# Sparse attention and a gated feed-forward layer: how the fourth tile's attention output is transposed, and the order of the work around it

## The chip, the cores and the metric

The kernel runs on one core of one Trainium2 chip. The metric is the device time of one execution in microseconds (us), lower is better. A core has a matrix engine (TensorE, PE in the profile; its weight loads are listed as PEld), two elementwise engines (VectorE, DVE; ScalarE, ACT), GpSimd (POOL), which here adds rows and issues the loads, and SyncE (SP), which issues DMA transfers. Each engine takes its instructions strictly in order; semaphores tie the engines together. Matrix products land in PSUM, everything else lies in SBUF.

## The reference

Attention over 4 batches, 8 heads, 768 positions of width 64, followed by a feed-forward layer on 3072 rows of width 512 (hidden width 2048):

```python
k_sum = k.reshape(B, H, nb, block, D).max(axis=3)      # blocks of 32 keys
v_sum = v.reshape(B, H, nb, block, D).mean(axis=3)
scores_l = scale * q @ k^T, kept only where |i - j| < 16
scores_s = scale * q @ k_sum^T + log(32)
a = softmax(concat(scores_l, scores_s))
attn = a @ concat(v, v_sum)
x = attn, heads side by side, as [3072, 512]
h = x @ w_in
out = (h * clip(h + 3, 0, 6) / 6) @ w_out
```

Inputs and output are float32; the kernel works in bfloat16 with float32 accumulation.

## The kernel before, in words

**Tiles.** The 3072 rows are eight tiles of 384 (s = 0 to 7: batch s // 2, half s % 2); "the fourth tile" is s = 3. For a tile the attention gives x, kept transposed in SBUF (`x`, 128 x 4 x 384: the width on the partitions), because the first product (`f1`, L703) needs it so. That product has 16 groups `F{s}x{ft}`: four matmuls into one of three PSUM accumulators `h`, then on ScalarE the clamp from below (L707), then on VectorE the upper clamp and the product with h, which writes `g` (L708) and frees the accumulator. The second product (`f2`, L720) takes `g` to the output: per 128 rows four parts `G{s}{ts}x0.0` to `.3` of four matmuls each into the one accumulator `o`, a copy to SBUF (`.4`) and a store by SyncE (`.5`).

**Attention of a batch.** Loads by GpSimd (`K`, `Q`, `V`, `H` and `B` entries); block transposes of keys and queries on VectorE (`turn`, L461 and L465), the block maxima (L473) and their spreading; value sums (`vsum`, `u` entries: for the later batches additions on GpSimd, L567, then spreads over the windows by ScalarE or VectorE); scores of half a batch for four heads at a time (`scores4`, L518: 48 small matmuls), the exponential on ScalarE (L526) and the mask on VectorE (L527).

**Value products and the transpose of x.** `values` (L646, entries `v{b}{half}{g}`, batches counted from 0: the fourth tile's are v110 and v111) makes for half a tile's width g the value products (`.0`, L660: 24 matmuls), the reciprocal of the sums (`.1`, L635) and the scaled rows `xn` (`.2`, L642). Then there are two ways to turn `xn` into x:

- tiles s < LATE: six identity matmuls on TensorE (`.3`, L673) into PSUM and one copy from there to x (`.4`, L247, by ScalarE or VectorE);
- tiles s >= LATE: VectorE transposes blocks of 32 x 32 in place of the whole (`.3`, L679) into `y`, and SyncE moves the blocks to their partitions: after both halves, four entries `.4` to `.7` of the second half g = 1, four transfers each (L685), sixteen for a tile. The tile's first products wait for all sixteen.

**What sets the order.** A list of 1000 entries written out by hand, ORDER, is walked from front to back; each entry emits one operation on its engine, and a letter behind a colon (A, D) picks ScalarE or VectorE where either could do it. Each engine so gets its own order, and buffers are given to whoever comes first in the list. [...]

Of the kernel before, what the change touches and what calls it, by code (L numbers as in the profile page):

```python
# [15 lines left out]
D = 64  # L16
# [27 lines left out]
F1x12.0 F1x12.1 F1x12.2 O0.0 G02x0.0 F1x10.0 F1x10.1 Q1w5.0 F1x10.2 Q1w3.0 O1.0 q4.0 q5.0 G02x0.1 F1x3.0 F1x6.0 q5.1:A q4.1:A  # L44
s100.0 F1x3.1 w13.0 F1x6.1 w12.0 F1x11.0 O2.0 s100.1 O3.0 F1x3.2 w12.2 F1x6.2 s100.3 w13.2 w12.3:D G02x0.2 s101.0 G02x0.3
s101.1 F1x13.0 G02x0.4:A V10.0 s100.2 s101.3 w13.3:A F1x0.0 G00x0.0 w12.1:D G00x0.1 V12.0 K20.0 w13.1:A h110.0:A s110.0 F1x0.1
Q22.0 s110.3 K22.0 s110.1 K21.0 s100.4 G00x0.2 K23.0 G00x0.3 s101.2 u4.0 G00x0.4:A h130.0:D Z.0 h100.0:D F1x0.2 s110.4 G01x0.0
G01x0.1 G01x0.2 B2.2 G01x0.3 s110.2 H2.0 Q20.0 u4.1:A Q23.0 u4.2:D u4.5:A u4.3:D F1x13.1 u4.4:D F1x11.1 F1x11.2 F1x13.2 v100.0
h120.0:A v101.0 v100.1 v100.2 G01x0.4:A v101.1 h131.0:A G12x0.0 v101.2 G12x0.1 G12x0.2 h121.0:A v100.3 w21.0 v101.3 v101.4:D
v100.4:A G12x0.3 h111.0:A s111.0 G12x0.4:A s111.1 w20.0 F2x1.0 F2x1.1 V22.0 h101.0:A B2.3 F2x3.0 F2x2.0 w21.3 B2.0 F2x3.1  # L50
G10x0.0 w23.0 F2x2.1 F2x1.2 w23.3 Q21.0 G10x0.1 s111.3 G00x0.5 F2x3.2 B2.1 w20.2:A F2x2.2 F2x14.0 w22.0 w21.4:A F2x5.0 G10x0.2
F2x14.1 F2x15.0 w23.4:A K30.0 V20.0 F2x5.1 F2x14.2 s111.2 F2x11.0 F2x15.1 F2x5.2 G10x0.3 F2x13.0 F2x11.1 s111.4 w23.2:A F2x15.2
F2x10.0 w22.2:A s101.4 u5.0 F2x11.2 F2x4.0 F2x13.1 K32.0 G10x0.4:A w20.3 v111.0 F2x13.2 v110.0 F2x4.1 w21.1 F2x4.2 v110.1
v111.1 F2x12.0 v110.2 v111.2 G11x0.0 G11x0.1 F2x0.0 F2x12.1 w22.1 K33.0 w20.1 w21.2:A F2x10.1 v111.3 F2x0.1 v111.4:A F2x0.2
u5.1 w21.5:A v110.3 u5.2 w20.5:A F2x12.2 v110.4:A u5.3 H2.1:A G12x0.5 G11x0.2 F2x10.2 G11x0.3 F2x8.0 u5.4 w20.4:A G11x0.4:A
G10x0.5 F2x6.0 F3x5.0 F2x6.1 Q30.0 u5.5 w23.1 F2x8.1 w22.3 F3x5.1 F2x6.2 s200.0 G22x0.0 u5.6 F2x8.2 F3x5.2 u5.7 s200.1 Q33.0
F2x7.0 u5.8 s200.3 F2x9.0 w22.4:D u5.9:D F2x7.1 F2x7.2 F2x9.1 u5.11:D s210.0 F2x9.2 F3x9.0 F3x14.0 G22x0.1 u5.12:D F3x13.0
s210.3 s200.2 s210.4 s210.1 F3x14.1 F3x9.1 G11x0.5 u5.10:A F3x14.2 F3x9.2 F3x13.1 G22x0.2 s200.4 Q31.0 s210.2 F3x13.2 F3x4.0
v201.0 v200.0 v201.1 F3x8.0 G22x0.3 F3x4.1 v201.2 G22x0.4:A F3x4.2 K31.0 Q32.0 v200.1 F3x7.0 v200.2 F3x12.0 F3x7.1 v201.3
G20x0.0 v200.3 s201.0 w23.5:A G20x0.1 F3x8.1 G20x0.2 F3x8.2 G20x0.3 F3x12.1 s201.1 w22.5:A s201.3 G20x0.4:A F3x12.2 F3x7.2  # L60
w30.0 B3.3 w31.0 F3x0.0 F3x2.0 F3x0.1 w30.3 G22x0.5 s211.0 F3x0.2 F3x3.0 B3.1 F3x2.1 G21x0.0 s201.2 w31.2:A v201.5 w33.0 F3x1.0
s211.1 F3x3.1 F3x1.1 F3x3.2 s211.3 G21x0.1 s201.4 F3x2.2 G21x0.2 F3x1.2 s211.4 F3x6.0 w31.3 F3x6.1 w30.2:A v201.6 G21x0.3
s211.2 w31.1 F3x10.0 F3x6.2 w33.3 H3.0 v201.4 F3x10.1 w31.4:A w30.4:A B3.0 B3.2 v211.0 v201.7 v210.0 G20x0.5 F3x11.0 V30.0
V32.0 G21x0.4:A u6.0 G21x0.5 F3x10.2 F3x15.0 F3x11.1 F3x15.1 F3x11.2 v211.1 F3x15.2 w30.1 G32x0.0 w30.5:D v211.2 G32x0.1 v210.1
u6.1 G32x0.2 w31.5:A H3.1:A F4x15.0 v210.2 F4x15.1 F4x7.0 G32x0.3 F4x4.0 F4x15.2 u6.2 F4x2.0 G01x0.5 F4x7.1 w33.4:D G32x0.4:A
F4x7.2 F4x2.1 F4x4.1 v210.3 F4x8.0 F4x8.1 v211.3 u6.3 F4x4.2 G30x0.0 G30x0.1 F4x2.2 F4x8.2 F4x6.0 s300.0 v211.6 w32.1 F4x6.1
v211.5 F4x14.0 u6.4 F4x14.1 F4x5.0 F4x5.1 u6.5 F4x6.2 w33.1 F4x13.0 F4x14.2 s300.1 G30x0.2 u6.6 w32.0 u6.7 F4x5.2 F4x3.0
F4x13.1 w33.2:A G30x0.3 F4x3.1 F4x12.0 u6.8 G30x0.4:A s300.3 F4x13.2 w32.2:D F4x3.2 w32.3 w32.4:D s300.2 F4x0.0 u6.11:D F4x0.1
F4x12.1 F4x11.0 F4x12.2 G31x0.0 u6.10:D w33.5:D G31x0.1 F4x11.1 s310.0 v211.7 u6.9:D F4x0.2 u6.12:D F4x1.0 F4x11.2 G31x0.2
F4x10.0 F4x9.0 s310.1 v211.4 w32.5:D F4x1.1 s300.4 s310.3 G31x0.3 s310.2 s310.4 F4x1.2 G02x0.5 F4x10.1 F4x9.1 v301.0 v300.0  # L70
F5x14.0 F4x10.2 F4x9.2 G31x0.4:A v301.1 F5x14.1 G30x0.5 v300.1 G42x0.0 v300.2 F5x5.0 F5x14.2 v301.2 v300.3 F5x2.0 F5x4.0 s301.0
F5x2.1 G42x0.1 F5x2.2 G42x0.2 v301.3 G31x0.5 F5x5.1 F5x9.0 s301.1 v301.7 F5x4.1 F5x5.2 F5x9.1 v301.6 s301.3 F5x0.0 F5x4.2
F5x9.2 F5x0.1 F5x6.0 s301.2 F5x0.2 G42x0.3 s311.0 F5x3.0 F5x6.1 F5x6.2 F5x1.0 s311.1 G42x0.4:D F5x3.1 G40x0.0 v301.4 F5x13.0
v301.5 F5x1.1 s311.2 F5x3.2 s311.3 F5x1.2 G40x0.1 s301.4 s311.4 F5x13.1 F5x10.0 v310.0 F5x13.2 v311.0 v310.1 v310.2 F5x7.0
F5x7.1 F5x7.2 v311.1 F5x8.0 F5x8.1 F5x8.2 F5x10.1 F5x10.2 G40x0.2 F5x12.0 G40x0.3 G40x0.4:A G42x0.5 F5x15.0 F5x11.0 v310.3
v311.2 v311.3 v311.7 F5x11.1 G32x0.5 G41x0.0 G41x0.1 G41x0.2 F5x11.2 F5x15.1 F5x15.2 F6x14.0 F5x12.1 F5x12.2 F6x14.1 F6x14.2
# [87 lines left out]
def kernel(  # L164
# [683 lines left out]
```

## Time and profile before

| what | value |
|---|---|
| time, median of 3 runs | 216.33 us (215.77 to 216.93) |
| the profiled execution's own time | 215.64 us |
| its span, first to last instruction | 213.9 us |
| PE busy | 207.7 us (97%) |
| DVE busy | 162.4 us (76%) |
| ACT busy | 131.2 us (61%) |
| POOL busy | 75.6 us (35%) |
| granted TensorE clock | 1.000 |

The profile is one execution. Busy time of an engine counts its instructions, not its waits on semaphores; matmuls overlap in the array, so from a timeline the price of a group of matmuls is read from the start of the group to the start of the next. The table by stretches gives each engine's busy time within a window. The chain of waits follows the work that ended last back to the front, and its pieces follow each other in time.

### The profile page before, as it was taken

Reading aid. Unit: us, or ns where it says so; the run is one execution under the profiler, and the core shown is the slowest. Engines: PE = TensorE matmul, PEld = TensorE weight load, DVE = VectorE, ACT = ScalarE, POOL = GpSimd, SP = SyncE. Lnnn points to the kernel's source line nnn. Section 1 sums busy time; section 2 is a strip of 40 time slices with the busy share of each in tenths; the row PEclk is TensorE's granted clock in tenths of the full one; section 3 lists DMA queues with packets and bytes.
Section 4 is the critical chain, followed back from the end, with each engine's and each line's share of the span. In section 5 each row is a group of like instructions: output and inputs, shape, how many; then the busy total and the mean of one; then the engine's idle time right before and its main releaser. Section 6 shows DMA issues by size and latency. Waiting matters only on the chain.

```text
span 213.9 us, 5917 instructions
## 1 busy us (share of the span) xinstructions
PE 207.7 (97%) x2444; PEld 118.4 (55%) x2444; DVE 162.4 (76%) x314; ACT 131.2 (61%) x266; POOL 75.6 (35%) x93
## 2 busy tenths in 40 slices
PE   7988999999999999999999999999999999999994
PEld 7556666655545555555555555555555555564443
DVE  6976999899199999999999999978865555650021
ACT  3869978888896867976664486375345355520110
POOL 7968358935743199980891000000000000000000
PEclk9999999999999999999999999999999999999999
DMA  5999999999999994899965033413314400113123
GB/s 76 157 155 187 204 187 171 190 204 163 183 196 182 193 164 43 115 178 167 171 57 161 9 39 44 134 16 39 72 21 78 78 0 11 41 49 123 52 82 139
DMA packets 92363, 24.23 MB, mean 113 GB/s; under 512 B 82480, under 2 KB 89008, under 8 KB 92336
## 3 DMA queue, kind: packets, MB, share of 16 engines
q0 software_dynamic: 62928, 15.99, 77.0%
q1 hardware_dynamic: 29264, 7.80, 16.2%
q8 instruction: 19, 0.31, 0.6%
q10 hardware_dynamic: 144, 0.07, 0.1%
q14 instruction: 8, 0.07, 0.1%
HBM read 31.97 MB, written 6.29 MB: 179 GB/s over the span
## 4 chain that ended last, share of the span: by engine, by line
PE 65%; DVE 24%; DMA 3%; ACT 2%; issue 2%; POOL 2%; DVEq 0%; POOLq 0%
PE h L703 29%; PE o L720 23%; DVE g L708 6%; PE h L720 5%; DVE at L527 4%; DMA first<-in_q_dram 3%; DVE kaug L461 3%; DVE xn L642 2%; DVE red L473 2%; DVE vaug L247 2%; DVE qT L465 2%; PE S L518 2%; PE S L660 1%; POOL first L311 1%; PE S L703 1%
## 5 line engine op out<-in xcount | busy, mean ns | idle before, releaser
L703 PE MATMUL h<-x,win 128*128 128x384 bf16 x500 | 92.2, 326 | 0.3
L707 ACT ACTIVATE r<-h 128x384 f32<-128x384 f32 x125 | 58.7, 491 | 42.1 <-PE h L703 40.0
L720 PE MATMUL o<-wout,g 128*128 128x512 bf16 x336 | 81.6, 379 | 0.0
L708 DVE SCALAR_TENSOR_TENSOR g<-r,h 128x384 bf16<-128x384 f32 x125 | 65.4, 544 | 18.2 <-ACT r L707 16.1
L703 PEld LDWEIGHTS <-win 128*128 128x128 bf16 x512 | 48.7, 98 | 36.6 <-issue 0.9
L720 PEld LDWEIGHTS <-g 128*128 128x128 bf16 x416 | 38.7, 98 | 37.5
L526 ACT ACTIVATE at<-S 120x768 bf16<-120x768 f32 x24 | 19.0, 810 | 4.2 <-PE S L518 4.2
L247 ACT COPY ot<-o 128x512 f32<-128x512 f32 x17 | 9.9, 585 | 16.5 <-PE o L720 16.3
L527 DVE TENSOR_TENSOR at<-at,mask 96x768 bf16<-96x768 bf16 x24 | 14.9, 645 | 0.5 <-ACT at L526 0.4
L642 DVE TENSOR_TENSOR xn<-S,rc 128x768 bf16<-128x768 f32 x14 | 13.2, 952 | 0.2
L247 DVE COPY ot<-h 128x512 f32<-128x512 f32 (+1 forms) x3 | 1.6, 554 | 14.3 <-PE h L720 14.3
L349 POOL DMA_DIRECT2D vaug<-in_v_dram x10 | 11.9, 1197 | 0.7 <-DMA qraw<-in_q_dram 0.4
L567 POOL TENSOR_TENSOR first<-first 128x512 f32<-128x512 f32 (+2 forms) x8 | 9.6, 1202 | 7.0 <-DMA first<-in_v_dram 6.4
L567 POOL TENSOR_TENSOR own<-own 128x512 f32<-128x512 f32 (+2 forms) x8 | 9.2, 1154 | 6.9 <-DMA own<-in_v_dram 6.5
L720 PE MATMUL h<-wout,g 128*128 128x128 bf16 (+2 forms) x80 | 11.4, 294 | 0.0
L473 DVE TENSOR_REDUCE red<-kaug 128x24 bf16<-128x768 bf16 x12 | 11.1, 928 | 0.0
L247 ACT COPY vaug<-vaug 32x640 bf16<-32x640 bf16 (+3 forms) x20 | 10.6, 579 | 0.8 <-ACT qT L247 0.7
L816 PE MATMUL o<-idle 128*128 128x64 bf16 (+2 forms) x71 | 7.4, 281 | 1.1 <-DVE idle L293 1.1
L461 DVE STREAM_TRANSPOSE kaug<-kraw 128x768 bf16<-128x768 bf16 x8 | 8.0, 1018 | 0.0
L660 PEld LDWEIGHTS <-at 120*64 120x64 bf16 x336 | 6.1, 111 | 3.1 <-issue 1.7
L518 PEld LDWEIGHTS <-kaug 32*128 32x128 bf16 x576 | 5.3, 92 | 4.4 <-issue 4.1
L679 DVE STREAM_TRANSPOSE y<-xn 128x768 bf16<-128x768 bf16 x8 | 7.5, 962 | 0.0
(117 smaller groups left out, 196.1 us busy)
## 6 DMA issues: line engine op xcount, KB each, us to landing
out_dram<-ot SPq DMA_DIRECT2D x19, 256.0 KB, 2.3
vaug<-in_v_dram POOLq DMA_DIRECT2D x6, 384.0 KB, 13.5
wout<-in_moe_w_out_dram POOLq DMA_DIRECT2D x4, 512.0 KB, 9.8
win<-in_moe_w_in_dram POOLq DMA_DIRECT2D x3, 512.0 KB, 9.9
kraw<-in_k_dram POOLq DMA_DIRECT2D x8, 192.0 KB, 11.0
x<-y SPq DMA_DIRECT2D x64, 24.0 KB, 2.1
first<-in_k_dram POOLq DMA_DIRECT2D x6, 192.0 KB, 13.5
first<-in_q_dram POOLq DMA_DIRECT2D x6, 192.0 KB, 10.6
```

The lines of the kernel that those rows point to most:

```text
L247: {"ACT": nc.scalar.copy, "DVE": nc.vector.tensor_copy, "POOL": nc.gpsimd.tensor_copy}[eng](o, i)
L349: op("POOL", "dma128", lambda: nc.gpsimd.dma_start(out=o[BLK:WIN, a:z, 0:D], in_=rows[:, a:z]), w=[("v", b % 2, c) for c in range(lo, hi)] ...
L461: op("DVE", "turn", lambda: nc.vector.transpose(out=w[:, :, BLK:WIN].rearrange("p t (r s) -> p t s r", s=2), in_=blocks_of(kraw[(b + 1) % ...
L473: op("DVE", "max", lambda: nc.vector.tensor_reduce(red.slot[:], w[:, :, BLK:WIN].rearrange("p t (n c) -> p t n c", n=2), axis=AX.X, op=ALU ...
L526: op("ACT", "exp", lambda a=a, e=e: nc.scalar.activation(a, X[e].slot[0:KEYS, :, 0:HALF], AF.Exp, scale=scl), r=[X[e]], w=[("at", p, half)])
L527: op("DVE", "masking", lambda m=m: nc.vector.tensor_tensor(m, m, mask[:, low(half):low(half) + HQ].unsqueeze(1).to_broadcast([WIN, 2, HQ, ...
L567: nc.gpsimd.tensor_tensor(o, x, y, op=ALU.add)
L642: nc.vector.tensor_tensor(o, src[..., 0:D], r.unsqueeze(len(r.shape)).to_broadcast(list(o.shape)), op=ALU.mult)
L703: nc.tensor.matmul(bank(h)[:, 0:HALF], w_in_sb[:, kt, cols], xt[s].slot[:, kt], start=(kt == 0), stop=(kt == NP - 1))
L707: op("ACT", "relu", lambda: nc.scalar.activation(r.slot[:], bank(h)[:, 0:HALF], AF.Relu, bias=0.5, scale=1.0 / 6.0), r=[h], w=[r])
L708: op("DVE", "gate", lambda: nc.vector.scalar_tensor_tensor(gt[s].slot[:, ft], r.slot[:], 1.0, bank(h)[:, 0:HALF], op0=ALU.min, op1=ALU.mul ...
L720: nc.tensor.matmul(o.slot[:, a:z], gt[s].slot[:, ft, ts * 128:(ts + 1) * 128], w_out_sb[:, ft, a:z], start=(ft == 0), stop=(ft == NFT - 1))
```

## The change

Two things change. `LATE` goes from 4 to 3, so the fourth tile's outputs go by VectorE's block transposes and SyncE's moves, as the tiles after it do already. And ORDER is replaced from its entry 271 (in the product groups of the second tile) to entry 799 (in the sixth tile); the entries before and after are the same. The table has 1002 entries now: the fourth tile loses two copies and gains four moves.

```diff
     NS = S // 128
-    LATE = 4
+    LATE = 3
     SPLIT = 5
...
-v111.1 F2x12.0 v110.2 v111.2 G11x0.0 G11x0.1 F2x0.0 F2x12.1 w22.1 K33.0 w20.1 w21.2:A F2x10.1 v111.3 F2x0.1 v111.4:A F2x0.2
...
+s111.2 v111.0 F2x2.1 F2x15.1 B2.3 H2.0 F2x2.2 F2x15.2 Q32.0 v111.1 v110.0 G12x0.4:A v111.2 v110.1 G10x0.0 v110.2 V22.0 v111.3
+F2x7.0 w21.2:A F2x11.1 F2x7.1 F2x4.0 G10x0.1 w20.2:A v110.3 F2x4.1 G10x0.2 F2x7.2 F2x11.2 G10x0.3 G10x0.4:A F2x10.0 F2x0.0
+F2x10.1 G11x0.0 F2x4.2 w23.0 u5.0 w20.3 u5.1 F2x6.0 F2x0.1 F2x10.2 w20.4:A H2.1:A G11x0.1 w21.1 F2x0.2 F2x12.0 G11x0.2 F2x12.1
+F2x6.1 w23.3 w23.2:A w20.1 u5.2 F2x9.0 u5.3 F2x6.2 G11x0.3 w23.4:A G12x0.5 F2x12.2 s200.0 w22.1 w22.2:A v111.5 v111.7 G11x0.4:A
+F2x9.1 F2x8.0 w22.3 v111.4 s200.1 s200.3 w22.4:A u5.4 u5.5 v111.6 u5.6 F2x13.0 G22x0.0 F2x8.1 u5.7 w23.1 G02x0.5 G01x0.5 u5.8
+F2x13.1 F2x9.2 u5.12:A F2x8.2 s200.2 G22x0.1 u5.9:D F2x13.2 w23.5:A u5.11:D s210.0 G22x0.2 s210.3 F3x5.0 F3x4.0 w22.5:A s200.4
...
```

In the lines with a plus, TensorE's part from the fourth tile's value products (v111.0, v110.0) to its first product (F3x5.0) is the entries G and F ending in .0 to .3 (G) or .0 (F), and s200.0 and s210.0.

On VectorE, around the fourth tile's two scalings (`rc` are the reciprocals, `xn` the scaled rows, `S` PSUM, `g` the gated products, `qT` the queries). Before:

```order
L708 SCALAR_TENSOR_TENSOR g_97<-r_108,h_93 128x384
L635 RECIPROCAL rc_113<-S_89 128x12
L635 RECIPROCAL rc_111<-S_90 128x12
L642 TENSOR_TENSOR xn_106<-S_89,rc_113 128x768
L642 TENSOR_TENSOR xn_104<-S_90,rc_111 128x768
L465 STREAM_TRANSPOSE qT<-first 128x12x2x32 x2
L708 SCALAR_TENSOR_TENSOR g_97<-r_109,h_93 128x384
```

and now:

```order
L708 SCALAR_TENSOR_TENSOR g_97<-r_107,h_92 128x384
L635 RECIPROCAL rc_113<-S_89 128x12
L642 TENSOR_TENSOR xn_106<-S_89,rc_113 128x768
L635 RECIPROCAL rc_111<-S_90 128x12
L642 TENSOR_TENSOR xn_104<-S_90,rc_111 128x768
L679 STREAM_TRANSPOSE y_102<-xn_106 128x6x4x32
L679 STREAM_TRANSPOSE y_102<-xn_104 128x6x4x32
L708 SCALAR_TENSOR_TENSOR g_97<-r_110,h_93 128x384
```

The two block transposes of `xn` into `y` stand right behind the scalings; the transposes of the queries come later.

On SyncE, the queue of stores (`out_dram<-ot`) and moves (`x<-y`). Before:

```order
L731 DMA out_dram<-ot_123 128x512
L731 DMA out_dram<-ot_121 128x512
L685 DMA x_98<-y_102 32x12x32 x16
L731 DMA out_dram<-ot_123 128x512
L731 DMA out_dram<-ot_121 128x512
L731 DMA out_dram<-ot_122 128x512
L685 DMA x_99<-y_103 32x12x32 x16
```

and now:

```order
L731 DMA out_dram<-ot_123 128x512
L685 DMA x_101<-y_102 32x12x32 x16
L731 DMA out_dram<-ot_120 128x512
L731 DMA out_dram<-ot_122 128x512
L730 DMA out_dram<-ot_121 16x512
L731 DMA out_dram<-ot_121 112x512
L731 DMA out_dram<-ot_123 128x512
L731 DMA out_dram<-ot_120 128x512
L685 DMA x_98<-y_103 32x12x32 x16
```

A set of sixteen moves, those of the fourth tile, now comes behind the first two stores; four store transfers that came ahead of all moves before follow it.

On GpSimd, the loads and the additions of the third batch (`own`). Before:

```order
L349 DMA vaug_77<-in_v_dram 64x48x64
L567 TENSOR_TENSOR own<-own 128x512
L339 DMA kraw<-in_k_dram 32x24x128 x2
L567 TENSOR_TENSOR own<-own 128x512 x4
L339 DMA qraw<-in_q_dram 32x24x128
```

and now:

```order
L339 DMA kraw<-in_k_dram 32x24x128
L590 DMA own<-in_v_dram 24x2x2048
L358 DMA vaug_77<-in_v_dram 32x95x64
L339 DMA qraw<-in_q_dram 32x24x128
L349 DMA vaug_77<-in_v_dram 64x48x64
L567 TENSOR_TENSOR own<-own 128x512 x7
```

The loads no longer stand between the additions; some are ahead of them, the rest behind.

More of the change, by code (lines that the diff above doesn't have):

```diff
@@ L47 @@
[L47 to L50, printed above, removed]
@@ L55 @@
[L55 to L58, printed above, removed]
@@ L59 @@
[L59 to L76, printed above, removed]
```

55 lines of the change are left out of this document (38 added, 17 removed).

## The prediction

> **What bounds the kernel now.** I read the page first, then the table by stretches, then the chain of waits, then TensorE's timeline. From the page:
>
> ```profile
> span 213.9 us, 5917 instructions
> PE 207.7 (97%) x2444; PEld 118.4 (55%) x2444; DVE 162.4 (76%) x314; ACT 131.2 (61%) x266; POOL 75.6 (35%) x93
> PE 65%; DVE 24%; DMA 3%; ACT 2%; issue 2%; POOL 2%; DVEq 0%; POOLq 0%
> ```
>
> TensorE is busy for 97% of the span, so a change gains only what it takes off TensorE's stream or out of its few waits. Yet a quarter of the chain is VectorE. The table by stretches (us, then busy time of PE, PEld, DVE, ACT, POOL, the granted clock, the DMA share and GB/s) says where:
>
> ```profile
> 66.00:74.00 8.00, 8.00 (x99) 4.53 (x97) 8.00 (x13) 7.45 (x17) 1.51 (x3) 1.00 1.64 194
> 90.00:98.00 8.00, 7.92 (x93) 4.53 (x87) 7.82 (x16) 5.54 (x10) 5.60 (x6) 1.00 1.69 171
> 80.00:84.00 4.00, 4.00 (x30) 2.15 (x28) 4.00 (x8) 2.66 (x7) 3.83 (x5) 1.00 0.32 42
> ```
>
> From 66 to 98 us VectorE is as full as TensorE, at the full granted clock, so there an edit that loads VectorE can reach TensorE. The unit prices on TensorE stand in the chain, where pieces follow each other without a gap (start, us, what):
>
> ```profile
> 128.97 1.73 PE o L720 x8
> 130.69 0.48 PE S L518 x48
> 131.17 0.76 PE h L703 x4
> 131.93 0.86 PE o L720 x4
> 132.79 1.30 PE h L703 x8
> ```
>
> One group of the first product (L703, four matmuls) costs 0.65, one of the second (L720) 0.86, one score pass 0.48, and a change from the full-size groups to a small kind and back costs 0.1 more (0.76 against 0.65). What is left above these prices is waiting. TensorE's timeline shows it in five places:
>
> ```profile
> 62.08 1.25 PE L660 MATMUL S<-vaug,at 120*64 120x65 bf16 x48
> 63.27 0.39 PE L720 MATMUL o<-wout,g 128*128 128x512 bf16 x1
> 75.99 2.42 PE L703 MATMUL h<-x,win 128*128 128x384 bf16 x12
> 78.34 0.82 PE L660 MATMUL S<-vaug,at 120*64 120x65 bf16 x40
> 93.67 0.81 PE L703 MATMUL h<-x,win 128*128 128x384 bf16 x4
> 94.56 1.00 PE L660 MATMUL S<-vaug,at 120*64 120x65 bf16 x48
> 95.50 0.82 PE L703 MATMUL h<-x,win 128*128 128x384 bf16 x4
> 111.30 1.72 PE L703 MATMUL h<-x,win 128*128 128x384 bf16 x8
> 112.86 2.75 PE L720 MATMUL o<-wout,g 128*128 128x512 bf16 x12
> 134.89 0.95 PE L660 MATMUL S<-vaug,at 120*64 120x65 bf16 x48
> 135.93 0.81 PE L703 MATMUL h<-x,win 128*128 128x384 bf16 x4
> ```
>
> Start to start: the value products at 62.08 take 1.19 where the pair at 94.56 takes 0.94, so 0.25 is waiting; the three groups at 75.99 take 2.35 against 2.05 (0.30); 93.67 takes 0.89 against 0.75 (0.14); 111.30 takes 1.56 against 1.31 (0.25); 134.89 takes 1.04 (0.10). Together 1.0 us: all that a better order can still take out of this part, and the only room that the order has.
>
> **The change part by part.** *Transposes removed.* In the fourth tile twelve identity transposes go, and one change of kind with them:
>
> ```profile
> 82.30 0.84 PE L673 MATMUL S<-ident,xn 128*128 128x128 bf16 x12
> 82.98 0.38 PE L720 MATMUL o<-wout,g 128*128 128x512 bf16 x1
> L247 ACT COPY x<-S 128x768 bf16<-128x768 bf16 x4 | 3.2, 802 | 2.0 <-PE S L673 2.0
> L679 DVE STREAM_TRANSPOSE y<-xn 128x768 bf16<-128x768 bf16 x8 | 7.5, 962 | 0.0
> L247 ACT COPY vaug<-vs 24x1536 bf16<-24x1536 bf16 x2 | 2.9, 1469 | 0.1
> L247 DVE COPY vaug<-vs 24x1536 bf16<-24x1536 bf16 x10 | 5.8, 584 | 0.3
> ```
>
> 82.98 - 82.30 = 0.68, plus 0.1: TensorE's stream is 0.78 us shorter. Counted over the whole rewritten part, the runs of small kinds go from 21 to 20, so "fewer changes of kind" is worth this 0.1 on TensorE and no more. The VectorE page of the Trainium skill (VectorE: DVE Perf Modes, Rules for kernel authors) speaks against the edit: it gives 128x128 transposes to TensorE wherever PSUM will do as the destination. Its table (The three transpose paths) has 390 ns for one on TensorE, by which twelve would be 4.7 us; the row gives 57 ns each in a stream, and the measurement decides.
>
> *VectorE and ScalarE.* The two copies from PSUM leave ScalarE (1.6 us) and two block transposes come to VectorE (1.9 us). Fifteen other entries that either engine could take change sides; the dearest are the spreads of the value sums: three go to ScalarE and one comes back, 1.2 us less for VectorE and 2.9 us more for ScalarE. The others are small copies, six going and five coming; by their count and the 584 ns above I bound their sum at half a microsecond either way and take it as -0.5, since the larger ones leave. VectorE's load is thus up by about 0.2 us in 45, and costs nothing while its results come before TensorE asks; ScalarE, at 5.54 of 8 us busy, hides its share. If VectorE falls behind, the first products wait for one of their three accumulators, as at 75.99.
>
> *The moves, and the room behind them.* This is the new wait. The sixteen moves of a tile follow both block transposes, one after the other on SyncE, and the tile's first product needs them all. What it takes, from the fifth tile, which goes this way already, and the seventh (the group of reciprocals; two rows of VectorE's timeline; the moves by stretch, with count, issue time in ns, first and last start, and their landing):
>
> ```profile
> L635 DVE RECIPROCAL rc<-S 128x12 f32<-128x12 f32 x14 | 2.9, 215 | 0.9 <-PE S L660 0.9
> 97.22 0.96 DVE L642 TENSOR_TENSOR xn<-S,rc 128x768 bf16<-128x768 f32 x1
> 98.09 1.83 DVE L679 STREAM_TRANSPOSE y<-xn 128x768 bf16<-128x768 bf16 x2
> L685 SPq DMA_DIRECT2D x<-y x4: 643/670/726, 100.0 to 102.2; - x4
> DMA to landing us min/median/max: 6.2/6.7/7.6
> L685 SPq DMA_DIRECT2D x<-y x4: 617/622/1146, 110.4 to 112.4; - x4
> DMA to landing us min/median/max: 2.0/2.5/3.1
> L685 SPq DMA_DIRECT2D x<-y x8: 592/618/619, 141.0 to 145.6; - x8
> L685 SPq DMA_DIRECT2D x<-y x8: 618/618/941, 146.3 to 151.4; - x8
> 115.45 0.81 PE L703 MATMUL h<-x,win 128*128 128x384 bf16 x4
> ```
>
> A scaling costs 0.87 from start to start, both block transposes 1.83. From the first to the last issue it is 10.4 us where the DMA engines are quiet (141.0 to 151.4) and 12.4 where they are loaded (100.0 to 112.4); the last lands 2.0 to 2.5 later. In the new order VectorE does nothing between the two scalings and the two block transposes, so from the end of the tile's value products: 3.7 (two reciprocals, two scalings, both block transposes: 0.4 + 1.74 + 1.83, less some 0.3 that the first half is ahead) + 0.1 + 10.4 to 12.4 + 2.1 = 16.3 to 18.3 us.
>
> The room is what TensorE does meanwhile. In the new entries 11 second-product groups, 9 first-product groups and 2 score passes stand between the fourth tile's second value product and its first product: 11 x 0.864 + 9 x 0.65 + 2 x 0.58 = 16.5 us (0.864 is 1.73 / 2). For the fifth tile it was 115.45 - 95.50 = 20.0, and nothing waited there. So the wait is between none and 1.8 us; with the middle of the two spans, 11.4, it is **0.8 us**, which I take. Behind that product stands all of TensorE and, through the accumulators, ScalarE's clamps and VectorE's gates; what VectorE owes is paid off meanwhile. Behind the moves on SyncE stand the stores of output buffers filled long before; they are asked for again only after this product, so they add nothing unless the moves come later still. The fifth tile's room shrinks from 20.0 to 18.5 (10 x 0.864 + 12 x 0.65 + 2 x 0.58 + 0.94); at 4.4 + 11.4 + 2.1 = 17.9 (4.4 is 95.50 to the end of the transposes at 99.92) that still fits.
>
> *Loads moved.* GpSimd now issues the loads of K and Q in another order, with 192 KB more issued before the pause that its first run of additions makes. At the 190 GB/s of the rows this fills the DMA engines 1 us longer than the fall to 42 GB/s in the stretch 80 to 84 us; the next load then waits for VectorE's last transpose of the third batch. The moves run from about 77 to 88 us: from 62.08 to the end of the fourth tile's value products the new entries have 0.94 + 4 x 0.864 + 0.78 + 0.58 + 7 x 0.65 + 1.04, which ends at 73.4, and 3.7 more is 77.1. So the first few meet the loads and the last do not. That is why 2.1 us for the last landing is taken.
>
> *Sum.* -0.78 (transposes), +0.8 (first product of the fourth tile), and half of the 1.0 us of present waits, -0.5, because VectorE gets 0.8 us to catch up at that point and the waits before and after it are in rewritten stretches: **-0.5 us**. The profiled execution took 215.64 us, its span being 213.9; that gives 215.1. The median of the runs shown, 216.33, is 0.7 above the profiled one, so I give 215.8.
>
> **The rivals.** *Moves in time.* If the moves issue at 0.66 us each throughout and VectorE is never late, there is no wait and the old ones go too: -0.78 - 1.0 = -1.8 us, 214.5. For it: the 10.4 us span fits the 16.5 us room to 0.2 us, and the end of the loads lies in the middle of the moves. Against it: three of the four sets had longer gaps (up to 1882 ns in one issue, below), and the order before still left 1.0 us.
>
> ```profile
> L685 SPq DMA_DIRECT2D x<-y x64: 585/618/1882, 100.0 to 167.8; - x64
> DMA to landing us min/median/max: 1.9/2.1/7.6
> ```
>
> *No change.* VectorE takes the block transposes in the stretch where it is full and hands on what TensorE saves: waits on the accumulators stay at 1.0 us or grow, and with 0.8 at the fourth tile the net is 0 to +0.3, 216.3 to 216.6. That the change does less than it says belongs here: TensorE changes its kind one time less in 21.
>
> *Slower.* The moves collide with the loads to their end. If the last move takes 6.7 us to land instead of 2.1 and the issues take 12.4 us, the first product waits 3.7 + 0.1 + 12.4 + 6.7 - 16.5 = 6.4 us; with 11.4 and a landing of 5 us it is 3.7. Less 0.78 and all of the old waits, the net is +1.9 to +4.6; I put it near 218.5, the lower end. It decides from a last landing of about 4 us. For it: the fifth tile's first four moves, issued among loads at 188 GB/s, took that long. Against it: the quiet stretch after 80 us. The DMA page of the skill (DMA: Bandwidth & Descriptors, Anatomy of one DMA — SWDGE (gpsimd) path) has about 2 us fixed per transfer plus bytes over 436 GB/s, which for 24 KB would be 2.06 us and leave this rival nothing; the quiet rows agree and the 6.7 us row does not.
>
> **How the numbers follow.** Forecast (wait of 0.8, half of the old waits gone) 0.45; moves in time 0.26; no change 0.16; slower 0.13. About 0.5%, or 1.1 us, is what a measurement of this kernel can tell from no change. Faster by more: the second case whole and a sixth of the forecast, 0.33. Slower by more: the last case and a third of "no change", 0.18. Within: 0.49. The range for 8 in 10 goes from just under the second case, 214.2, to 217.4, which leaves out most of the collision; the forecast's own range is 215.0 to 216.6 (wait between 0 and 1.6).
>
> **What would show it.** Right: no L673 in the fourth tile, a gap of 0.3 to 1.5 us before TensorE's first L703 of that tile near 90 us, put down to the moves; landings near 2 us for the last moves; the end of TensorE's stream about 0.5 us earlier. Wrong: no gap there (second case), landings above 4 us there (collision), or new gaps at other L703 groups put down to VectorE's L708.

## The result, and the profile after

The changed kernel takes 222.78 us (median of 4 runs, 221.9 to 223.93) where the kernel before takes 216.09 (4 runs, 215.77 to 216.93) beside it: a ratio of 1.0307 with a 95% interval of 1.0249 to 1.0365. It is slower by 6.7 us. The forecast was 215.8 with a range of 214.2 to 217.4, and the case that came, a collision of moves and loads, had a chance of 0.13 and a price of 218.5. The profiled execution took 221.9 us, 1.7 more than its span. Runs that lie over 1.5% above the fastest of their kernel are left out of the ratios below; it is one run, at 223.7 us, of the kernel with idle matmuls. From the page of the changed kernel:

```profile
span 220.2 us, 5916 instructions
PE 208.9 (95%) x2432; PEld 117.9 (54%) x2432; DVE 162.6 (74%) x312; ACT 132.4 (60%) x268; POOL 74.8 (34%) x93
PE   7898999999999999399996999999999999999994
PEclk9999999999999999969999999999999999999999
PE 70%; DVE 12%; DMA 8%; SPq 4%; issue 1%; ACT 1%; POOL 1%; DVEq 0%; POOLq 0%
```

Twelve matmuls are gone, as predicted, yet TensorE is busy for longer (208.9 against 207.7 us). The page cuts the span into 40 slices of 5.5 us: TensorE has a hole in the 17th and a smaller one in the 22nd, and its granted clock is down in the 18th. The chain now has SyncE's queue and DMA in it and half of VectorE's share. TensorE's timeline around the first products of the fourth and the fifth tile:

```profile
89.11 1.04 PE L720 MATMUL o<-wout,g 128*128 128x512 bf16 x4
93.78 3.81 PE L703 MATMUL h<-x,win 128*128 128x384 bf16 x12 [3.63 <-DMA out_dram<-ot]
97.42 0.82 PE L720 MATMUL o<-wout,g 128*128 128x512 bf16 x3
118.34 1.04 PE L720 MATMUL o<-wout,g 128*128 128x512 bf16 x4
120.99 2.11 PE L703 MATMUL h<-x,win 128*128 128x384 bf16 x12 [1.61 <-DMA out_dram<-ot]
```

Counted from start to start, with the 0.864 of the prediction for the group of the second product that stands ahead: the fourth tile's first product was due at 89.97 and came at 93.78, 3.8 us late. Its first three groups then took 97.42 - 93.78 = 3.64 instead of 3 x 0.65 = 1.95, 1.7 us more. The fifth tile's first product was due at 119.20 and came at 120.99, 1.8 us late. The releaser named is a store that ended last by the profile; the stores stand behind the moves on SyncE, and these products read no store, so the moves have to be looked at. Their issues by stretch (count, issue time in ns as minimum, median and maximum, first and last start, then the landing in us after the start of the issue): the first, second and last four of the fourth tile and the last four of the fifth.

```profile
L685 SPq DMA_DIRECT2D x<-y x4: 611/624/728, 77.3 to 79.4; - x4
DMA to landing us min/median/max: 3.6/4.0/5.1
L685 SPq DMA_DIRECT2D x<-y x4: 618/620/620, 80.1 to 82.1; - x4
DMA to landing us min/median/max: 2.0/2.4/3.1
L685 SPq DMA_DIRECT2D x<-y x4: 618/618/619, 85.4 to 87.4; - x4
DMA to landing us min/median/max: 6.1/6.4/6.6
L685 SPq DMA_DIRECT2D x<-y x4: 618/620/637, 113.9 to 115.9; - x4
DMA to landing us min/median/max: 2.0/3.8/5.0
```

The last four moves of the fourth tile, 24 KB each, land 6.1 to 6.6 us after their issue, near 93.8, where the first product starts. What lies beside them is in GpSimd's timeline and in the table by stretches (busy time of PE, PEld, DVE, ACT, POOL; clock, DMA share, GB/s):

```profile
84.47 0.46 POOL L567 TENSOR_TENSOR vs<-own 128x128 bf16<-128x128 f32 x1
84.87 0.64 POOL L590 DMA_DIRECT2D first<-in_v_dram  x1
85.50 0.72 POOL L339 DMA_DIRECT2D kraw<-in_k_dram  x1
86.22 1.34 POOL L349 DMA_DIRECT2D vaug<-in_v_dram  x1
```

```profile
82.00:84.00 2.00, 2.00 (x13) 1.08 (x11) 2.00 (x4) 1.70 (x4) 1.84 (x3) 1.00 0.40 41
90.00:92.00 2.00, 0.15 (x1) 0.00 (x0) 1.91 (x5) 1.09 (x4) 1.30 (x3) 1.00 2.03 141
92.00:94.00 2.00, 0.22 (x2) 0.16 (x3) 0.45 (x1) 0.00 (x0) 0.09 (x1) 1.00 1.77 245
94.00:96.00 2.00, 2.00 (x8) 0.93 (x7) 0.38 (x1) 0.90 (x2) 0.00 (x0) 0.50 1.67 232
96.00:98.00 2.00, 2.00 (x9) 0.89 (x7) 1.66 (x4) 1.16 (x3) 0.00 (x0) 0.65 1.34 294
98.00:100.00 2.00, 2.00 (x56) 1.32 (x54) 0.91 (x3) 1.28 (x4) 0.00 (x0) 1.00 1.71 202
```

GpSimd issues its next loads as soon as its additions end, from 84.87 us on, while the last four moves are still to be issued. And after nearly four idle microseconds TensorE runs at a granted clock of 0.50. In stretches of 0.1 us it is 0.50 from 94.0 to 97.4 us and 1.00 from there on; the 0.65 in the table is the mean of the two.

Theory: **the moves land among loads, TensorE idles, and its clock falls.** Rivals: the new order is slow in itself (VectorE's gates late: a gate is the product L708, which writes `g` and frees an accumulator); the single SyncE queue is too slow for sixteen moves; the transposes' removal costs more than it saves.

### The profile page after: what moved, and what is told of

It is laid out like the page before. It is cut to its first block, busy times and chain, and to the rows that moved or that the text cites. A ratio compares the mean times of both kernels' runs of the same rounds, so it can differ in the third digit from the quotient of the medians.

```text
span 220.2 us, 5916 instructions
## 1 busy us (share of the span) xinstructions
PE 208.9 (95%) x2432; PEld 117.9 (54%) x2432; DVE 162.6 (74%) x312; ACT 132.4 (60%) x268; POOL 74.8 (34%) x93
## 4 chain that ended last, share of the span: by engine, by line
PE 70%; DVE 12%; DMA 8%; SPq 4%; issue 1%; ACT 1%; POOL 1%; DVEq 0%; POOLq 0%
PE h L703 31%; PE o L720 25%; PE h L720 5%; DMA out_dram<-ot 5%; SPq L685 4%; DVE g L708 4%; DMA first<-in_k_dram 3%; PE S L660 2%; DVE xn L642 2%; PE S L518 2%; DVE y L679 2%; DVE at L527 1%; DVE kaug L461 1%; PE S L703 1%; PE S L495 1%
## 5 line engine op out<-in xcount | busy, mean ns | idle before, releaser
L703 PE MATMUL h<-x,win 128*128 128x384 bf16 x500 | 93.7, 330 | 5.6 <-DMA out_dram<-ot 5.2
L708 DVE SCALAR_TENSOR_TENSOR g<-r,h 128x384 bf16<-128x384 f32 x125 | 65.4, 543 | 23.7 <-ACT r L707 21.9
L703 PEld LDWEIGHTS <-win 128*128 128x128 bf16 x512 | 49.2, 99 | 43.7 <-DMA x<-y 4.1
L247 ACT COPY ot<-o 128x512 f32<-128x512 f32 x18 | 10.5, 586 | 18.7 <-PE o L720 18.6
L527 DVE TENSOR_TENSOR at<-at,mask 96x768 bf16<-96x768 bf16 x24 | 13.4, 571 | 1.3 <-ACT at L526 0.9
L679 DVE STREAM_TRANSPOSE y<-xn 128x768 bf16<-128x768 bf16 x10 | 9.5, 963 | 0.1
L247 ACT COPY vaug<-vaug 32x640 bf16<-32x640 bf16 (+3 forms) x17 | 8.2, 548 | 2.1 <-DMA vaug<-in_v_dram 1.4
L339 POOL DMA_DIRECT2D kraw<-in_k_dram x8 | 5.7, 721 | 8.5 <-DVE kaug L461 6.7
## 6 DMA issues: line engine op xcount, KB each, us to landing
win<-in_moe_w_in_dram POOLq DMA_DIRECT2D x3, 512.0 KB, 10.9
kraw<-in_k_dram POOLq DMA_DIRECT2D x8, 192.0 KB, 12.3
```

The costliest lines, as they stand in the source:

```text
L247: {"ACT": nc.scalar.copy, "DVE": nc.vector.tensor_copy, "POOL": nc.gpsimd.tensor_copy}[eng](o, i)
L527: op("DVE", "masking", lambda m=m: nc.vector.tensor_tensor(m, m, mask[:, low(half):low(half) + HQ].unsqueeze(1).to_broadcast([WIN, 2, HQ, ...
L679: op("DVE", "blocks", lambda: nc.vector.transpose(out=ys[s].slot[:, :, 6 * g:6 * g + 6].rearrange("p a m i -> p m a i"), in_=xn.slot[:].re ...
L703: nc.tensor.matmul(bank(h)[:, 0:HALF], w_in_sb[:, kt, cols], xt[s].slot[:, kt], start=(kt == 0), stop=(kt == NP - 1))
L708: op("DVE", "gate", lambda: nc.vector.scalar_tensor_tensor(gt[s].slot[:, ft], r.slot[:], 1.0, bank(h)[:, 0:HALF], op0=ALU.min, op1=ALU.mul ...
```

## The experiments

Every kernel below computes the whole of the reference; where something is added, it is said. In kernels with an added line above, the numbers of lines are one higher (L704 is L703). In the cuts from ORDER, three dots stand for entries left out.

**The new order with TensorE's transposes.** `LATE` back to 4; the moves and block transposes of the fourth tile go, its two transposes come back.

```diff
-    LATE = 3
+    LATE = 4
- v111.3 ... v110.3 ... v111.5 v111.7 ... v111.4 ... v111.6
+ (after G10x0.2) v111.3 v110.3 v111.4:A v110.4:A
```

> The changed order, but the fourth tile transposed on TensorE again and copied by ScalarE, so it has no moves. Theory (the last four moves of the fourth tile land among loads and TensorE, idle for 3.8 us, then runs at a lower clock for some 4 us): the wait before the tile's first product and the slow groups behind it go, 3.8 + 1.7 us, and the transposes come back, 0.8; the fifth tile's wait of about 1.8 us stays. 222.8 - 5.5 + 0.8 = about 218, granted clock 1.00. Rival (the new order itself is late on VectorE, whichever way the tile is transposed): waits appear in other places and the time stays above 220.

Measured: 217.47 us, ratio 1.0056 (1.0028 to 1.0084). That is near the expected 218. So 5.3 of the 6.7 us came with the way of transposing, and the order without it costs 1.2 us. Its longest waits in TensorE's timeline are three for VectorE's gates and one, at the fifth tile's first product, that is still put down to moves:

```profile
89.88 1.04 PE L720 MATMUL o<-wout,g 128*128 128x512 bf16 x4 [0.43 <-DVE g L708]
111.00 0.81 PE L703 MATMUL h<-x,win 128*128 128x384 bf16 x4 [0.47 <-DVE g L708]
112.20 0.81 PE L703 MATMUL h<-x,win 128*128 128x384 bf16 x4 [0.39 <-DVE g L708]
116.23 2.11 PE L703 MATMUL h<-x,win 128*128 128x384 bf16 x12 [0.51 <-DMA x<-y]
```

**All loads behind the additions held.** A copy of two elements on GpSimd, added ahead of B3.3, reads the fourth tile's first gate, so that every later load starts after it.

```diff
+    plan.at("P3")
+    op("POOL", "hold", lambda: nc.gpsimd.tensor_copy(held[:], gt[3].slot[:, 5, 0:2]), r=[("g", 3, 5)], ...)
- B3.3
+ P3.0 B3.3
```

> The changed kernel with one small GpSimd copy ahead of the loads that follow the first run of additions; it reads a result of the fourth tile's first product, so those loads start only after it. Everything else as changed. Theory: the last moves land in about 2.1 us, so by 89.6 us; the first product starts near 90 us without a wait, the clock stays 1.00, and the time falls by 3.8 + 1.7 = 5.5 us to about 217.3 (a little less if the fifth tile's wait of 1.8 us goes too, as the loads behind it shift). Rival (sixteen moves are too many for the room, loads or not): first product still at 92 us or later, time above 220. Rival (the held loads are missed by the next batch): the wait returns at the scores or block transposes of the fourth batch, 219 or more.

Measured: 219.73 us, ratio 1.0162 (1.0116 to 1.0208). The moves of that stretch now land in 2.0 to 3.5 us, and the wait at the fourth tile's first product is gone; but a wait of the same size stands further on. The landings of the moves issued from 84.8 to 87.5 us, TensorE's row, and from the page VectorE's transposes of keys:

```profile
DMA to landing us min/median/max: 2.0/2.8/3.5
106.11 2.37 PE L704 MATMUL h<-x,win 128*128 128x384 bf16 x8 [3.52 <-DVE g L709]
L462 DVE STREAM_TRANSPOSE kaug<-kraw 128x768 bf16<-128x768 bf16 x8 | 8.2, 1027 | 4.6 <-DMA kraw<-in_k_dram 4.6
```

TensorE waits for a gate, and on VectorE this gate stands behind a block transpose of the last batch's keys, for which VectorE sits idle for 4.6 us (it starts at 104.16). These keys come with K31 and K30, issued at 93.3 and 95.4 us instead of 85.5 and 87.6: in the chain of this run the load of K has 10%. The clock falls again behind this idle time, to 0.68 and 0.50 in the two stretches from 106 to 110 us. The hold moved the wait from the moves to the keys, as the second rival had it. The first half of the theory stands; the expected time does not. Stores are no rival here: SyncE issues two of 256 KB right behind the moves in this run too (from 88.2 us; 88.0 in the change), and the last move, issued at 87.5, lands in 2.0 us.

**TensorE kept busy.** Sixteen idle matmuls are added ahead of the fourth tile's first product.

```diff
- F3x5.0
+ ~16 F3x5.0
```

> The changed kernel with 16 idle matmuls of 512 columns (16 x 0.22 = 3.5 us of TensorE) just before the fourth tile's first product, that is inside the wait of 3.8 us. Theory (the slow groups after the wait, 1.07, 1.28 and 1.28 us in place of 0.65, come from TensorE having idled): the three groups take 0.65 again, granted clock 1.00, and the time falls by about 1.7 us to 221. Rival (the lower clock there comes from something else, such as the transfers under way): the groups stay slow, 222.8 or a little more.

Measured: 221.09 us (median of all four runs), ratio 1.0219 (1.0166 to 1.0272): 1.7 us less than the change by the medians, 1.9 by the ratios. The twelve matmuls that took 3.81 us take 2.12, with the clock at 1.00 throughout the stretch:

```profile
93.92 2.12 PE L703 MATMUL h<-x,win 128*128 128x384 bf16 x12 [0.58 <-DMA x<-y]
```

So the fall of the clock is a consequence of the idle time and costs 1.7 us by itself (3.81 - 2.12). The Trainium skill (TensorE: Matmul & The Clock Gate, Part 1: The HAM clock gate) says that half the clock is granted after an idle window of about 3.4 us and the full one after as much sustained work. Its length agrees: 0.50 from 94.0 to 97.4 us in the change. The idle time ahead of it does not agree in every run, and there the measurement decides: the clock fell 3.8 us after the end of TensorE's last matmul in the change, but 2.6 us after it in the run with two queues and 1.8 us after it in the run with two loads ahead, both below. Behind the wait of 1.6 us at the fifth tile it did not fall.

**Half of the moves on ScalarE's queue.**

```diff
-                    nc.sync.dma_start(
+                    (nc.scalar if s == 3 and a > 1 else nc.sync).dma_start(
- v111.5 v111.7 v111.4 v111.6 (each at its own place)
+ (after v110.3) G12x0.5 v111.4 v111.6 v111.5 v111.7
```

> The changed kernel with the fourth tile's sixteen moves shared between SyncE and ScalarE's queue, eight each, both beginning when the block transposes are done. Theory: the last is issued near 82.5 us instead of 87.4, before the loads that start at 84.9, lands by 85 to 86, and the wait of 3.8 us and the 1.7 us of low clock go: 217.3, plus what eight issues cost ScalarE (at 0 to 0.6 us each, 0 to 5 us of an engine that is half idle there, so at most some 2 us on TensorE): 217.3 to 219.3. Rival (the wait is for the number of moves in flight or for VectorE, not for loads): first product still after 92 us, 222 or more.

Measured: 224.77 us, ratio 1.0404 (1.0361 to 1.0448). ScalarE's timeline shows why:

```profile
77.94 7.55 ACTq L685 DMA_DIRECT2D x<-y  x8
85.60 0.49 ACT L707 ACTIVATE r<-h 128x384 f32<-128x384 f32 x1 [8.82 <-DMA x<-y]
```

Eight issues hold ScalarE for 7.55 us: each takes 0.59 to 0.82, and between the fourth and the fifth lie about 2 us in which SyncE issues nothing either. No clamp and no copy runs in that time, and TensorE idles 6.3 us in front of an accumulator; the clock falls here too. The moves themselves land in 2.0 to 4.9 us, as the theory had it. A second queue is no remedy when its engine has work of its own.

**Two loads ahead of the additions u6.** V30.0 and H3.0 go from behind u6.6 and u6.7 to behind B3.2.

```diff
- u6.6 ... V30.0 u6.7 ... H3.0 u6.8
+ B3.2 V30.0 H3.0 ... u6.0 ...
```

> The change, with two loads of the last batch's values (V30.0 and H3.0, which the order gives to GpSimd among the additions u6) moved ahead of these additions. Theory (the fifth tile's last moves land late because these two loads are issued beside them, at 114.1 and 116.1 us): the last four moves of the fifth tile land in 2.0 to 2.4 us instead of 2.0 to 5.0, the wait of 1.6 to 1.8 us before its first product goes, the fourth tile's wait stays: 221.0 us. Rival (the fifth tile's moves are late because SyncE issues them late, or because the stores of the output stand in their way): the wait stays, 222.8 us. A third possibility is a loss: the two loads, now issued near 92 us, slow the fourth tile's last moves by up to 1 us more: 222 to 223.5.

Measured: 221.61 us, ratio 1.0211 (1.0157 to 1.0266). At the fifth tile's first product no wait is left, and its last moves land in 2.0 to 2.1 us: the theory holds there. At the fourth tile the wait is 4.9 us, more than in the change, since the issue of its moves took 12.3 us (two single issues of 1.4 and 1.5 us); the two loads, issued from 92.7 us on, came after that and did not cause it. The net is 1.2 us of the 1.8.

**Four loads ahead of the additions u5.**

```diff
- u5.8 ... B3.3 ... K31.0 V32.0 ... K30.0 ... Q30.0 ... Q31.0
+ V22.0 K31.0 K30.0 Q30.0 Q31.0 ... u5.0 ...
```

> The change, with four loads of the last batch's keys and queries (K31, K30, Q30, Q31) moved from behind GpSimd's additions u5 to ahead of them, into 4.2 us in which GpSimd waits for data anyway. Theory (the bytes that are in flight beside the last moves set their landing): 0.79 MB of what stands among the last moves is gone, and 1.3 MB or so (the values) stays, so the last moves land in 3 to 5 us instead of 6.1 to 6.6, the wait of 3.8 us falls to 1 to 2.5, with a shorter or no fall of the clock: 218.5 to 221 us. Rival (any load beside the moves costs the same, the first of them decides): the landings stay at 6 us, 222.8 us. The first moves, at 77 to 80 us, may land later than now; they have room.

Measured: 223.4 us, ratio 1.0304 (1.0248 to 1.036): no gain, and the expected landing of 3 to 5 us missed. The last three moves now land in 8.4 to 9.5 us and TensorE waits 7.5 us. The loads ahead slowed the first moves (6.0 to 6.4 us to land). The last three were issued up to 1.6 us later, at 87.6 to 89.0, behind two single issues of 1.5 us, and so V32 and most of the four B3.x had been issued ahead of them. In this run fewer loads in total were no help, because more of what was left came ahead of the last moves.

**The early loads, a hold on the rest, and V30, H3 ahead.** The two edits above, and the hold of the second run ahead of B3.3.

```diff
+ V22.0 K31.0 K30.0 Q30.0 Q31.0 ... u5.0 ... u5.8 ... P3.0 B3.3 ... V32.0 ... B3.0 B3.1 ... B3.2 V30.0 H3.0 ... u6.0
```

> The change, with the four loads of keys and queries ahead of the additions u5, the four loads of values (B3.x) and V32 held until the third chunk group of the fourth tile has passed its gate (as in the run that held all loads), and V30.0 and H3.0 ahead of the additions u6. Theory (the whole loss is moves that land among loads, and loads that come late where they are held; nothing in the order itself costs over 1 us): no wait over 0.6 us is left at the first products of the fourth and fifth tile nor at the scores of the last batch, the clock stays at 1.00: 214.3 to 215.7 us, below the kernel before. Rival (the new order has waits of its own that the moves only covered, as the run with TensorE's transposes left them): 216.5 to 218 us.

Measured: 217.28 us, ratio 1.0048 (1.0018 to 1.0077). The clock stays at 1.00, and 5.5 of the 6.7 us are back, but the time meant is missed by 1.6 us. Two waits are left in TensorE's timeline, at the first products of the fourth and the fifth tile:

```profile
91.01 2.12 PE L704 MATMUL h<-x,win 128*128 128x384 bf16 x12 [0.89 <-DMA x<-y]
116.05 2.11 PE L704 MATMUL h<-x,win 128*128 128x384 bf16 x12 [1.32 <-DVE g L709]
```

The second has two causes that end together: the gate it is put down to ends at 116.05 us, and the fifth tile's last move, issued at 114.0, lands near 116.0.

**Fewer loads before each set of moves.** K31 and K30 alone go ahead, Q32, Q30, Q31 and B3.x behind the hold, and V32, V30 and H3.0 behind a second hold, on the fifth tile's first gate (F4x4). What the expectations call the third chunk group is, in the code, the gate that a tile makes first: F3x5 for the first hold, F4x4 for the second.

```diff
- H2.0 ... Q32.0 ... V22.0
+ H2.0 K31.0 ... V22.0 K30.0
+ P3.0 B3.3 ... B3.0 B3.1 ... B3.2 Q32.0 Q30.0 Q31.0 ... u6.0 ... u6.8 P4.0 V32.0 V30.0 H3.0
```

> The change, with GpSimd's loads placed so that next to none lies beside a move: K31 and K30 stand where Q32 and nothing stood, ahead of the additions u5; the four B3.x, Q32, Q30 and Q31 wait for the third chunk group of the fourth tile; V32, V30 and H3.0 wait for the third chunk group of the fifth tile. Theory (the 0.9 and 1.3 us of wait that the run with all three moves still shows are loads too: 0.79 MB more ahead of the first moves, which stretched their issue from 10.7 to 12.3 us, and V32, V30 and H3.0 ahead of the fifth tile's moves, which stretched theirs from 11.6 to 14.0 us): both issues take 10.5 to 11.7 us, no wait over 0.5 us at the two first products: 215.0 to 216.0 us. Rival (waits of the new order itself fill the place): 217 us or more, as before.

Measured: 217.42 us, ratio 1.0049 (1.0028 to 1.0071): missed; the rival's time. The fifth tile's moves are quicker (12.6 us for 16 issues; 14.0 in the run before, 11.6 in the change), the fourth's still take 12.3, with 0.87 us of wait behind them, and two waits of 0.7 us are put down to VectorE's gates. So neither the moves nor the order's own waits were done with.

**The loads where the prediction had put them.** The hold reads what VectorE's last transpose of the third batch writes.

```diff
+    op("POOL", "hold", lambda: nc.gpsimd.tensor_copy(held[:], qT[:, 3, PAD:PAD + 2]), w=["held"])
- B3.3
+ P3.0 B3.3
```

> The change, with the one dependence that the prediction had wrongly assumed: GpSimd's first load after its additions (B3.3) waits for VectorE's last transpose of the third batch (near 87.6 us), so that all loads start 2.5 to 2.8 us later than they do. Theory (it is the loads' start that the prediction had wrong, and a move's landing grows with what is in flight while it is): the last four moves land in 2 to 4 us instead of 6.1 to 6.6, the wait before the fourth tile's first product falls from 3.8 to 0.5 to 1.7 us, the clock falls less or not, the fifth tile's wait of 1.8 us stays: 217.8 to 220 us. Rival (the prediction would have been as wrong with the loads where it put them, since the moves' last landings are late in any case or a short overlap is enough): a wait of 3 us or more, 221.5 to 223 us.

Measured: 220.59 us, ratio 1.0183 (1.0135 to 1.0231), between the two. GpSimd's first load, the last five moves with their landing, and TensorE:

```profile
88.76 0.66 POOL L591 DMA_DIRECT2D first<-in_v_dram  x1 [0.33 <-issue]
L686 SPq DMA_DIRECT2D x<-y x5: 617/619/1398, 85.2 to 88.6; - x5
DMA to landing us min/median/max: 2.0/3.0/5.2
93.89 3.80 PE L704 MATMUL h<-x,win 128*128 128x384 bf16 x12 [3.25 <-DMA x<-y]
```

The last move was issued at 88.6 us, 0.2 ahead of the first load, and still took 5.2 us. So loads need not be ahead of a move to slow it: it is enough that they start while the move is under way.

**The hold where the last moves land.** It reads the third tile's gate F2x13 (near 90.7 us); the keys come first behind it, and nothing is added ahead of the moves. V32, V30 and H3.0 stand behind the second hold, as above.

```diff
+ F2x13.2 P3.0 ... K31.0 K30.0 B3.3 B3.0 B3.1 B3.2 Q30.0 Q31.0 ... u6.0 ... u6.8 P4.0 V32.0 V30.0 H3.0
```

> The change, with GpSimd's loads held from the third chunk group of the third tile's last gate but one (near 90.8 us, when the fourth tile's last moves land) instead of the fourth tile's first gate, in the order K31, K30, B3.3, B3.0 to B3.2, Q30, Q31; nothing is added ahead of the moves; V32, V30 and H3.0 wait for the third chunk group of the fifth tile. Theory (the moves' issue was stretched to 12.3 us by the loads of keys set ahead of it; without them it is 10.7 us again): no wait over 0.3 us at the fourth tile's first product; the keys are there in time for the scores, unlike in the run with all loads held to 92.3 us; the two waits for VectorE's gates near 111 and 116 us (0.7 us each) stay: 216.2 to 217.0 us. Rival (the keys come late again, and the wait goes to the scores of the last batch): a wait of 1 to 2 us there, 217.5 us or more.

Measured: 215.95 us, ratio 1.0005 (0.9976 to 1.0033), a little below what was expected. The first load, the moves with their landing, and what is left on TensorE:

```profile
91.17 1.49 POOL L340 DMA_DIRECT2D kraw<-in_k_dram  x2
L686 SPq DMA_DIRECT2D x<-y x5: 619/624/1332, 84.9 to 88.2; - x5
DMA to landing us min/median/max: 2.0/2.9/3.4
114.75 2.11 PE L704 MATMUL h<-x,win 128*128 128x384 bf16 x12 [0.72 <-DVE g L709]
```

The first load starts 2.4 us later than in the run before, the wait at the fourth tile's first product is gone, and so is the clock's fall; the scores do not wait for keys. **Against the change, the place of the loads alone is worth 222.78 - 215.95 = 6.8 us** (6.5 by the ratios), all that was lost, with all sixteen moves on one queue.

**The gates first.** On VectorE four gates of the fourth tile go ahead of a masking, a transpose, a maximum and two reciprocals, and one spread goes to ScalarE.

```diff
- w31.4:D ... G21x0.4:A s211.2 F3x3.2 ... w33.0 w30.3 ... F3x15.2 ... v211.1 v210.1 ... F3x10.2 F3x11.2 F4x4.0
+ w31.4:A ... G21x0.4:A F3x3.2 s211.2 ... F3x15.2 ... w33.0 ... F3x10.2 F3x11.2 w30.3 v211.1 v210.1 ... F4x4.0
```

> The run with the earlier hold, and on VectorE four gates of the fourth tile (F3x3.2, F3x15.2, F3x10.2, F3x11.2) ahead of a masking, a transpose, a maximum and two reciprocals that stood before them, and one maximum's spread (w31.4) on ScalarE. Theory (what is left of the new order's loss is VectorE, which is late with gates near 111 and 116 us because transposes and maxima of the last batch's keys stand ahead of them): both waits of 0.7 us go, 1.0 to 1.4 us less than the run with the earlier hold: 214.9 to 216.0 us. Rival (VectorE is full in this stretch, so that what is moved behind the gates makes the next piece late): the same time as the run with the earlier hold, within 0.4 us, with a wait of 0.5 us or more elsewhere between 105 and 125 us.

Measured: 214.79 us, ratio 0.9939 (0.9918 to 0.9959), 1.2 us less than the run with the hold and 0.6% faster than the kernel before. Of the two waits meant, the run with the hold still had 0.2 and 0.7 us, and both are gone; at the fourth tile's first product 0.7 us stand in this profiled execution, the longest of the twelve (215.6 us), where the issue of the moves took 12.5 us. VectorE's timeline of the run with the hold, then of this one:

```profile
112.39 1.03 DVE L462 STREAM_TRANSPOSE kaug<-kraw 128x768 bf16<-128x768 bf16 x1
113.33 0.90 DVE L474 TENSOR_REDUCE red<-kaug 128x24 bf16<-128x768 bf16 x1
114.16 0.54 DVE L709 SCALAR_TENSOR_TENSOR g<-r,h 128x384 bf16<-128x384 f32 x1
```

```profile
111.72 0.55 DVE L709 SCALAR_TENSOR_TENSOR g<-r,h 128x384 bf16<-128x384 f32 x1 [0.93 <-ACT r L708]
112.19 1.04 DVE L462 STREAM_TRANSPOSE kaug<-kraw 128x768 bf16<-128x768 bf16 x1
```

The gate that TensorE's accumulator waits for stood behind 1.8 us of work on the last batch's keys, and now stands ahead of it, where VectorE even idles for 0.93 us.

**One load among the moves.** The run with the hold, with K31 alone issued right after the additions.

```diff
+ u5.8 K31.0 ... P3.0 ... K30.0 B3.3 ...
```

> The run with the earlier hold, with one of its held loads (K31, 0.19 MB) issued right after GpSimd's additions, near 84.5 us, as in the change; all others stay held. Theory (a move waits behind the bytes that are in flight ahead of it): the moves issued within some 2 us behind that load land in 2.5 to 4 us, those after it in 2.0, and the last, issued near 88, in time: the time of the run with the earlier hold within 0.5 us, 215.7 to 216.5 us. Rival (any load among the last moves, however small, makes them land in 5 us or more): a wait of 2 us or more at the fourth tile's first product, 218 us or more.

Measured: 216.29 us, ratio 0.9998 (0.9971 to 1.0024). The expected time came and the rival's did not: one load of 0.19 MB, issued at 83.6 us, costs nothing here, and the first product starts at 90.04, 0.25 us late. The three moves issued from 83.9 to 85.2 us land in 3.7 to 4.2 us, and those of 83.5 to 84.9 in the run with the hold in 1.9 to 2.3. This is not shown to be the load's doing: in the run that held all loads, where the first starts at 92.7, the moves issued at 84.2, 84.8, 85.5 and 86.2 land in 4.0, 3.5, 3.0 and 2.6 us with no load in flight. That the amount in flight decides fits the runs above, but is not shown.

## Why the prediction was wrong, step by step

- **Transposes removed, -0.78 us.** The twelve matmuls are gone (2444 to 2432). In the run that puts them back they take 0.67 us from start to start, against the 0.68 of the prediction. No run takes this saving by itself.
- **Room and issue of the moves.** Right: the block transposes were to end at 77.1 and the first move is issued at 77.3; the last issue starts at 87.4, 10.1 us later, against 10.4 to 12.4 (10.1 to 12.3 in the runs that leave the moves on SyncE); the first product was due at 89.97, 16.5 us behind the value products.
- **Loads moved. This is the step that failed:** "the next load then waits for VectorE's last transpose of the third batch. [...] So the first few meet the loads and the last do not. That is why 2.1 us for the last landing is taken." The first load, B3.3, did not wait for that transpose but started at 84.87 us, when the additions ended, and the landing was 6.1 to 6.6 us. What it waits for on VectorE is the second of the four query transposes and not the last: in the run with two queues, where VectorE is late, it starts at 92.34, behind the second, which ends at 92.04, while the last starts at 94.95. In the change the second had ended at 84.04. And there was a second error under the first: in the run that forces the wait I had assumed, the loads start at 88.8 and the landing is still 5.2 us. I had compared the loads' start with the moves' issue, where it has to be compared with their landing: safe was a first load at 91.2 us, not at 88.8.
- **The wait at the fourth tile, 0.8 us.** It was 3.8, for that reason alone.
- **What follows an idle TensorE** was in no term: 1.7 us at a clock of 0.50, as the run with idle matmuls shows.
- **The fifth tile "still fits".** It did not: 1.8 us, since V30.0 and H3.0 are issued among its last moves (landing up to 5.0 us). With the two loads ahead, the wait is gone. The 0.6 us between 18.5 and 17.9 rested on the same 2.1 us: the landing took up to 5.0, the transposes ended 5.0 us behind the value products instead of 4.4, and the issue took 10.9, 21.0 us in all where the room was 19.3.
- **Half of the old waits gone, -0.5 us, and VectorE's load "costs nothing".** Wrong in sign for the order by itself: with the old transposes it is 1.2 us slower than before, some of it the fifth tile's moves (0.5 us of wait there), and rearranging VectorE's queue near 110 and 115 us in the run with the hold gave 1.2 us back. In the changed kernel itself these waits hardly show (0.7 us near 114); that TensorE's lateness gave VectorE time to catch up is the likely reason and is not tested.
- **The slower case** had the right place and mechanism; its wait of 3.7 to 6.4 us holds the 3.8. Its price of 218.5 left out the clock and the fifth tile, and its chance of 0.13 rested on the quiet stretch after 80 us of the kernel before, where the additions end later.

The sum by the changed kernel's rows: 3.8 + 1.7 + 1.8 = 7.3 us of new loss, and a further 0.7 in two short waits in TensorE's timeline near 114 us, less 0.78 and the 1.0 of old waits, which TensorE's timeline no longer has: 6.2, where the spans differ by 220.2 - 213.9 = 6.3.

## What to carry to other kernels

When work moves from a compute engine to small transfers that a product waits for, draw up the issue times of every other queue's loads against the time at which the last transfer must have landed, not against its issue, and take the landing among loads, not the quiet one, wherever they overlap. Price a long wait on TensorE with the slow clock behind it: here the clock fell in or behind every wait of 3.25 us and more, and not behind those of 1.6 us and less. A load that is held back must have its own due time looked up first: holding all of them only moved the wait to VectorE, which needs the keys.

## What the runs showed of the hardware that was not expected

- A 24 KB move that lands in 1.9 to 2.1 us at best takes 6.1 to 6.6 us beside the loads of the change and 8.4 to 9.5 us among V32 and the four B3.x; a move issued 0.2 us before the first load took 5.2 us. Some are late without a load: four of them took 2.6 to 4.0 us in the run that held all loads.
- TensorE's granted clock fell to 0.50 between 1.8 and 4.1 us after the end of its last matmul (1.8 in the run with two loads ahead, 2.6 with two queues, 3.3 with the loads where the prediction had put them, 3.8 in the change, 4.1 in the run that held all loads; in the last three, work had just begun again), and was back at 1.00 between 3.1 and 5.7 us after its work began again (5.7 in the run with four loads ahead). Behind a wait of 1.6 us it stayed at 1.00.
- ScalarE issues a move in 0.59 to 0.82 us and SyncE, in the same stretch of the same run, in 0.59 to 0.72.
- In ten of the runs one of the last moves takes 1.0 to 1.6 us to issue, also where no load is in flight (1332 ns in the row above). In each of them the profile has a transfer of 0.02 MB on a queue of instructions (q8) that begins within 0.4 us of the start of that issue, ahead of it in nine of the ten; in the change it comes at 88.8 us, after the last move, and none of the last moves is slow to issue. A second issue of 1.4 to 1.6 us, near 81 us in five of these runs, has no such transfer beside it. No edit tested this, and the cause is open.
